# Two groups of six PSUM banks in place of three groups of four, in the second stage of a long-convolution transform

## The chip, the cores and the metric

The kernel runs on one core of one Trainium2 chip. The metric is device time in microseconds (us): from the start to the end of one execution. The engines are TensorE (PE in the profile; PEld is its weight loads), VectorE (DVE), ScalarE (ACT), GpSimd (POOL) and SyncE (SP), which issues all transfers. Matrix products go to PSUM, eight banks of 512 float32 per partition, and are copied from there to on-chip memory by ScalarE or VectorE.

## What is computed

The kernel computes the output and all gradients of a layer that adds three things: its input, a gated long convolution, and a gated bilinear unit. The sequence has 2048 tokens of 512 features, and everything is bfloat16.

```python
xn = layernorm(A_q)
k_shift = sum(pad(k)[:, t:t+S] * shift_k[:, 3-t] for t in range(4))
kv = k_shift * v
y  = irfft(rfft(kv, 2*S) * rfft(ssm_k, 2*S))[:S] + kv * ssm_D
out = A_q + xn * y + ((xn @ w_gate) * (xn @ w_up)) @ w_down
# returned: out, and its gradients by A_q, A_k, A_v, A_shift_k, A_ssm_k,
# A_ssm_D, w_gate, w_up and w_down for a given grad_out
```

The convolution over 2048 tokens needs three transforms forward: of the filter K, of kv, and of dy = xn * grad_out. Three products of these, frequency by frequency, give y, the gradient of kv and the gradient of the filter, and each of them is transformed back.

## The kernel before

**The transforms as matrix products.** Each transform is done in two stages. `a_gen` (line 432) does the first stage for all tokens, with a 64-row table, and stores the result to a scratch tensor AX. `s_gen` (line 543) then runs eight iterations over AX, two blocks each. One iteration has these parts:

- `s_load` brings in two blocks, each [128, 2, 3, 512]: the 3 are the signals t (K, kv, dy).
- `s_B(i)` (line 493) is the second forward stage. It multiplies pieces of 64 rows with tables of 64x32, for each of the two parts cp (real, imaginary), four column quarters q and two blocks s: 48 matmuls of 512 columns in all. A matmul of 64 rows and 32 columns uses an eighth of the array, so eight of them can lie side by side.
- `s_pw(2i)` and `s_pw(2i+1)` (line 508) form the three complex products on VectorE, ten operations for each block, from X (real and imaginary parts of the three signals) to Y.
- `s_Bi(i)` (line 525) is the inverse stage: three groups of 16 matmuls of 32 rows and 64 columns into four banks each, copied by ScalarE.

Later `last_dft` (line 687) does the last inverse stage.

**Groups and banks.** `rF()` asks for a tile of two adjacent banks, `rN()` for one bank. The lines between `together()` and `apart()` become a single operation for the order: the matmuls of a group are issued back to back. In `s_B` before, a group belongs to a signal t: two tiles `px[s]`, one for each block, hold its real and imaginary part, which makes four banks. Two copies empty them (line 505). ScalarE does both, except in the first iteration, where VectorE takes one of the two.

**Buffers.** There are three X tiles and six Y tiles, taken in turn: block b uses X[b % 3]. The X tile of a block is used again three blocks later.

**Other work.** Around these stages the same engines do the gated unit and its weight gradients. `mlp_rows` (line 400) forms the hidden units, with three PSUM tiles per call, each copied away. `dw_gen` (line 561) accumulates weight gradients, 16 matmuls in one bank before one copy. These matmuls stand between the groups of `s_B` and `s_Bi`.

**The order.** No scheduler runs on the chip's side. Every call is first recorded as an operation with a due time (`at`), and `emit(PLAN)` (line 181) issues all of them in an order that is written into the string PLAN, together with the bank of every PSUM tile. A planner made that string beforehand. Unpacked, it holds 2335 operation numbers and 411 bank numbers before. Each engine works through its own part of the order strictly in sequence, so a wait of one operation holds up all behind it on its engine.

Of the kernel before, what the change touches and what calls it, by code (L numbers as in the profile page):

```python
# [17 lines left out]
S = 2048  # L18
D = 512
F = 1376  # L20
R = 16
# [6 lines left out]
NCH = 8  # L28
# [1 line left out]
RING = 28  # L30
RO = [0, 16, 24, 40, 56, 72]
EPS = 1e-5
PLAN = "c-l>O0}w4u4`tF(-)GylZQHhO+qP}nwr$(C&AspYcdK@~dMcfq&dJQwbdtCLK)@iNVBjGDAs{4#g3u5K!a_WV1L+|l#E00B7;-=YKu82RAs6I@q>vkuKpqGO$ss&MfQXO}B0*$`0{Ni`M1^P&9b!NMC<v*c5EO-C5EIHnENB9SAsG~h3Q!YDKvO6QwV*Uqfs{}i%0MZo1a+V;q=l+b7V1G|XaHlNKD32~kOF!@H7Ez|U?4PtR8SEHK?`UPjbSh}gG|r?hCp@b2+46M^nsQz3_8IG=mMP~4Wz)4&<lpcRA>&Ppesy+`Opfc!)V9=-Cza$hLqSBQsE3p2P@$%^oCWi5PCvCm<fv^EA)r%Fbj^tY*++yU<s^-36L3D!x~rsYhfwOg^92p#z8n)2V-G3WQ2LJ0kXp$*aUlFJY<1wun{IhHrNNRVHxa))VLW=!U6aN$KVi5g5z)yw!>f80w*Ah{DD(&7y!4z9XJQ4;Ru|88?Xb;!d*y%h__$>T!Ni&8*aiqcmVgo;RSdDmx1sjoQJRQ4$>myMM#I~F$2B_!5sJ!a^h8Z1QGESJb^1<_z-g82bhSDVHd>4r|=oBLvDNydGHxrgN&${3BN&JoP?S26Xe4$kOi~i56Fg*F$`wM&6pp<V*!kU1+fqo#;6z$i(paoSPW}pag2sxaXLoF5;y~6U>&TB^{_rRz=jyWnAiwIVI*vfO>hfNfu`6DLt=CM4s9S7w!jy#6(?g$41sZQH@3l6*c#hnJ8X~JFf?|+jyMJ5;&vR532+B?!p^u6yI@z`i4(9J#>4K|7f)e7oQ*Sa7tX;R7$5uNN$iQou^0BnJva*o;AtF)eJ~;J#WPp~2H^o*f@g6s4#5aG4Ts`>9ENjoDxSloxCV#g2poy~@I02n1vn2E;UygHM&W2&jAL*ij&Y@NEv~?^xC~d}Sho_(U|C#^<uDPh$8|W)mB+-m2`k`u*VHv}NpOPe<St-RtcVw}r5ouwyXBY+-?`?ll`Dx8-9hZ&TDXO-nQP}-yN+&=>*?CK_HMDejJ@0vR|&6SWxR@2uqsx=D_9+CU`@R3y1QC<7jNJ=?BVWVe0Lvj<1HNJ61WHW5Fg=Ve1ZwxQ+$Tk@j1T0m-q@_;~RX7@9;f-z>jznKjCNmf?x3)E_L7W2mZuF?iVI@NnBEw%q4dzTuQghrE+)h5N^Pg?l=CyzX<LyqU-9MBgamhI&<CyTnHD^g>s=?7#G$pci~)k7r{kzkz8aK#T~(@E}Dz(Vz>-0rc3S8xU}w$%jjacOfIvl<c?xxm&FxyU0ha|&1H90++A1IRddx{4VS|ea)sRrm(CS&vE2}N&)sx6T`u<%a=ScksJrj-x_mCbi{nmUQCG~Rcg0;zH_4T7aa~Eb97?&;u8b?|%DD%wysO~myIQWctK;grimslk?~Y*s*T6k=4c%(j$h~*H-8vUmCc7zafLrVOxHWE&```w;ovxo7?E1Q?Zn)d!w!3L=y4&YwxMA*q+u>%q{cfw<?GCz+ZkF5TKDk3~j$7d7y7lh3n~#UxXE)oOc6;1Wcha43^W0;1#%*wq+$pDY)@^pT+&SlIliTR7IHMzOi~HsR#5BTPbs^}b`{MRGp-b+Sd+nmpWfzj(xC`#9i%v1<t-I*HyO@-ne!3qn2j!$(l$(CJ&~(jRcX{ZE`|ZL|JeQYNx##Yg%SZXC0EMTgE*2G}LKJ}t(+l^<MWNsULq+JXD@su*KE<X<<fyHiK#ko3nn;srCQYHR6kdu^LJCI_BoalGaTJl_QX(2p2`CvQr+ActQc@~PLW}5zn@Xvv7IkxpsWvU9g;a;?(k!Y+X{b1*rF4{@GEfXzLa`*K%%(^(hcePqiXzh~vSgxVw322}RGCMaDYitDxwMv65m9}LE~{xB9djiqu4JLC6h}%?Y05@rs4OLva#Wt;Nd>A%m8ddhl=zZB8c=_iSTajPszOz%5hayO(wH_;BB@5zDTy?pKD36iNHR$-O(~nypuW_P`cn$2NzG^gHK(kSU0P5Y$t5|YC8d&q6pB*IAR0{Rq!kUJp_G({QA)`v!zqJ|p!||nN>FPmC~YXc<d%^%ib~07Dj;pC9Tk%GG=|#K2I@dXq$72ra<Y$>Q(-AB^<+PFrY=-pHdA?NAbDg9b)~#gM!HdVDl0vxCsmNGluwFDMQI|HWE&Ni%5s2;N)>4)C1g9DcTJ_5Jfo`eoDNb$*+DO;xipfOR9#+CNqJ2*<PFu7UerR~Qf+xhz3DxDpvF>HK2jU$A!F$iIcO`N=?i_Oos^o>a4q>pX*nIYla^9Peo%L5CFwZ>XXH%WS~Bx4YA?Mc3wM;Bl9jV@Z^_R6<R^8IUo=|!N)8?)Ik}Vcmt5ROPEr>cAY-Mg43yv0S^m&pIz`=Nq6`w?$#Rs2$s|EOPRD4l<Yvc1Wt^O#AwqnHCdd?F&dXC}xQv&Xl8=RF%Lq}9L&gPpq|B00GM`S9=Q*-O3h^GAD~BjQ&y&3r;KLM>3-AtEDo5xl?UZX&mW%K%xlSwP2Hm7`e2b>Z3W>!tWSQKiJ5-qO(sH>+A^1M6l11`>D)Mw$D63^7t&xXxo+|NtStko*w_Kn{v_baDV~Wk2Bo42YxV%T=@fLYP<$1k4rF~L?FVaRiC<kP#ES9shU#8J^SwY(*6vyXFbdD16VL2p~xe7PrBXXHGOF}*>iTDZ?<%`mYL-R=~#>M%xT$03mO6v1vxgue>1SjF^a!eZV4XMk=<*Hnhq<lh>@l7eo_4t;&mUB{y@5mWR&Tl0wpOtW&g3n7zejsloJV&M%Qku(f1Wv^f`JP1LmlBz8OI3a)PvwzB;k)uqo=Z(`%<tuiJd|frop;k?iORM3gWQ)I+=M&w1^FbXZTX|r=4f1vqjM+zEbX`@e-Tp982nY*vuR(B$=`wrr2~uR;pbe3zsq;(!k4)p|B%l7OZxKw4(LE;y~3?{5dRj{Ncw{RNJxFjKP8GbXRnbptcK9RJcLbJa8!N8f8{EN)@b^aLuq(z%F*>1htr`PL&NAWZq2bZrVi(3+?BmV&{+D0zw>Lp#t}7+{@^w|g5&8(?#4YirN-6n+>29bA`M6n{>q6pjlSh1`i=YWC?3sYIJL&tvD}+K@;gqbY4ts)*94ke)9H22s5kfnXV9CRObh5IPNA9gCnwc{8bUJZ0=~t+IIG^~EV_^jX<og<`E?QJ)Wy7nKl4(~r^`5-7S`;#oO5fyis}l^p({C;hLlyjnv3XN{=&sHyshC9dXFpXeO}A!xVWz8lA1>!a1|}B5BU*~<MF(KCva5_VH3HUPU6QrnQQ12uBBzPrjnG?Iy#l>=`?1ksMC1{m(@dDNl|KR11+U9xw_8cCOVtvaCx1}b@ebG;R-sBkMgl#X>gq9b0a;$C%K`9wo_bRPxBdWrW?7jwo;Kz9LCycT06^4^&J1<kanIga0I)^zqzem;?3M%yJ%PKrrou*_RyZ%OMB}UZl}$4E4R>SwvD&*4*tt6wWIFjUBO1@u6EMh+(A{|>OJkOdw8gZmSH+vN9ai1%lr7g?&m&wfct7cJ;?oafWFg#I!GVuVBM*^bcpWOhx$bK=yQFldv%{a)BSotSLjN8p{w+uzSKv0NLTA99j#+@td7%Ac35BQ6F#D$WW2u72|7{3*(5!xuXM6b(Xh5gkLgrBu50yyp3rr=UN`7Qjc6xzlP0zVwppj^4BeuUY^$Eq(|ShFY8*SKk?p)*(5QA%FX?5yqDkzkUeoJ(LuYDI`>4t7rpB=M`bp#4ERAKeb&kfi4;t6LYjm5d^E93%vRgV|7idEJq1$x3MzMvuNEhog-JvOLiI%dImf4nS8e67WY`JE)WOiF~TL~*;sjQ-vv(i?{%Gyt@V3jSS{n9*^&Z<}@%WCPZq?u*2)Rx!0-O+s3%*tDH%WtEsl~uFxR=}!TK@-bmHLQ@;w6T`MYFS|$XFaX96|tiBS*zLv8)J3si~iQOhE~k#+H}ilf3&IfwRYCe+S?54VD+qp^|y}J)w)@Cn`Aw#flaph*2!jCL+fm6Uv-N0vTxeb2G~>^ZO$6mK$~X8t+5TVS=Pk{TN9gYZET3ev^h4^CfYC?Zu@Mh&9&Ax!uH!TTVTs=p3S#~cEDCxZ#!t~?X>l=>$c8z*<amYHw<i}ZL>u-(pK7b+hm7qv8}cpcGfoAO*?0|Y^NQzOSZ)>+8H}yw{5E(wIz1Pj@xBBW^3%cU9k*y*P{4mcEY0it9H_MTQvXN_E>a(!QNSD5B|Nqu)T)<f!(uT!BYFaJv8#K?UAwnV5dxcIDgH)*(&>JVf=Sf|Hfkawf4y(`XBb$o?0yb#bW!%_SMW+@lPzg59@zh93SxBhwyRzOAG0%`k(gJ;`u)o!&md^eF~r7NAU4|0iVGa^cj62U)?A0g?%Pp#Q(LFzNpXaBl%Rmn9uGL`Vu~o&+XIt96pp!>~s28R?{c(xqNb8#;5beeJx+oNA_8KZC}bK^>ut!U)N{zd3+6@+Sl{Re0fh+&gb>rJzIU>-&gcKd<Wm$_w)_?WMA3m^A&s=Kft%}4Sjn*(D(9Fd`I8d5AvP-RA1UR@`L>}-^6$JLwrj=)DQEO{0QI55BE*|3_sGh^)vk_-`e-~vwRmn+n4oS{d7OU&+*NCH$T_+@#FknKhKZx`}}yn-!Jp?{Q=+4xAUX@LEpyr^$Y!SzrY{z>-<)K*e~+i{1Ly{Z})5c1AojP^*j7Tf84L|>-`D8#BcBq{Yrn*Z}gA+PQS)K_N)9kf7@^JPyASa#!vE3{bqm1Kl5AsUBAmO^`HG}|J>j6r~DWH!teI?{a1h5zw$5rH-E{$_80wk|HfbTKm1!CGqA^B@gV{~eXPJ$A1(09M-Tk**L=vpZy!4lDsa|c_n`wZ0yq3$A0}|#Lx2Kd1MfTr!Uf(3Tea|k51s=Te8fP6fCO&(NP$~k191Y810THwKKUpCABY+V1V{x8nOyMi<zPN=YQg?M!Po(V8YqKf5(}DGIhe`W=|7u82qF;;gFPZB$bW_)I*5m$r{Kbr7=pc|ss*#X`=|fsG`MCFGnJq==<q*vu*HObuwe1W#uRiGEDbqGYk~qwgz|5XC<dv5^<Z$J{O=OhV9-HV!SRoV&Hk?x6iogh$cX~{NA+J6LFqp}_mB3U?DT*0KWk9?|4sf6_22lP?SI<fo&R6d8q@}Z4U#%kN9KaTss%y8Ac_7xZ;)6F{_SE5z7GZn1{PcdWBtcq!4L4yS@5_CqLJ8w-U<H?9`mRC"
KB = 1024


# [1 line left out]
def kernel(  # L38
# [39 lines left out]
    Q = [PP[:, 1024 * i:1024 * i + 1024] for i in range(4)]  # L78
    halves = [Q[i][:, 512 * h:512 * h + 512] for i in range(4) for h in range(2)]

    def v3(ap, a):
        return ap.rearrange("p (a b) -> p a b", a=a)
# [32 lines left out]
    def rF(kind="F"):  # L115
        slots.append(Slot(2, kind))
        return PV(slots[-1], lambda b: b)
# [86 lines left out]
    ACOPY = nc.scalar.copy  # L204
    VCOPY = nc.vector.tensor_copy
    MM = nc.tensor.matmul
# [37 lines left out]
    rW = Region(108 * KB, 132 * KB)  # L244
# [5 lines left out]
    W2 = W12[:, 128:192]  # L250
# [8 lines left out]
    c2 = rc.tile("c2", [128, R], F32)  # L259
# [205 lines left out]
    sp = {}  # L465

    def s_alloc():
        m = Region(RA[0] + 8 * KB, RA[1])
        sp["a"] = [m.tile(f"sa{i}", [128, 2, 3, D]) for i in range(3)]
        sp["X"] = [m.tile(f"sX{i}", [128, 3, 2, D]) for i in range(3)]  # L470
        sp["Y"] = [m.tile(f"sY{i}", [128, 2, D]) for i in range(6)]
        sp["T1"] = place([128, 2, 2, D], BF, RA[0])
        sp["T2"] = m.tile("sT2", [128, 2, 2, D])
        sp["C"] = [m.tile(f"sC{i}", [128, 2, 3, D]) for i in range(2)]
        sp["E"] = [m.tile(f"sE{i}", [128, 512]) for i in range(3)]

    def e_tab(i):
        return sp["E"][i % 3][:, 0:256].rearrange("p (g c k) -> p g c k", g=4, c=2)
# [12 lines left out]
        return 2 * s + q // 2, (q + s) % 2  # L491

    def s_B(i):
        for t in range(3):
            px = [v3(rF(), 2) for s in range(2)]
            together()
            for cp in range(2):
                for q in range(4):
                    for s in range(2):
                        g, j = s_pair(s, q)  # L500
                        h = slice(64 * j, 64 * j + 64)
                        MM(px[s][32 * q:32 * q + 32, cp, :], lhsT=e_tab(i)[h, g, cp, :], rhs=sp["a"][(2 * i + s) % 3][h, g % 2, t, :], start=True, stop=True)
            apart()
            for s in range(2):
                (VCOPY if i == 0 and s else ACOPY)(sp["X"][(2 * i + s) % 3][:, t, :, :], px[s])
            yield

    def s_pw(i):
# [50 lines left out]
    f = {}  # L559
# [228 lines left out]
    A0, AJ = 6.0, 38.0  # L788
# [3 lines left out]
    O0, OJ = 230.0, 10.0  # L792
# [60 lines left out]
    A = Gen(a_all())  # L853
# [41 lines left out]
    for n in range(NCH):  # L895
        last = n + 1 == NCH
        t = F0 + n * DF
# [138 lines left out]
```

## Time and profile before

| | before |
|---|---|
| time, median of 3 | 433.36 us (433.06 to 433.58) |
| span of the profiled execution | 1105.1 us |
| transfers | 123.07 MB, 34.4% of the DMA engines' time in the span |
| copies of 128x1024 from PSUM on ScalarE | 155, mean 1016 ns |
| copies of 128x1024 from PSUM on VectorE | 13, mean 1224 ns |

The profiled execution is one of the program on the chip, but it took 2.55 times as long as the timed ones. What it shows of a single operation of VectorE or ScalarE, and of the sequence on each engine, is of use; shares of the span have to be read with that ratio in mind. A group of instructions in the profile shows line, engine, operation and shape, then count, total busy time and the mean of one in nanoseconds, and last the idle time before these instructions with what ended it. Since a helper issues everything, all lines are line 173, and the groups are told apart by shape: 64x512 with a 64\*32 table is `s_B`, 32x512 with 32\*64 is `s_Bi`.

### The profile page before, as it was taken

The page shows a single profiled execution, that of the slowest core. Times are in us where ns is not written, and L with a number is a line of the kernel's source. Part 1 is how long each engine was busy: PE and PEld are TensorE (multiplying, and loading weights), DVE is VectorE, ACT ScalarE, POOL GpSimd, SP SyncE. Part 2 cuts the span into 40 slices and gives each one's busy share as a digit, 9 for nine tenths or more (in the row PEclk, how much of TensorE's full clock was granted, in tenths as well). Part 3 has the DMA queues.
Part 4 walks back from the last instruction along what each step waited for, and adds up shares of the span by engine and source line. Part 5 has one row for each costly group of instructions (what it writes and reads, how often), then busy time and mean ns, then how long its engine had stood idle before and what let it go on. Part 6 is the DMA issues. An engine that isn't in the chain of part 4 may idle for free.

```text
span 1105.1 us, 8192 instructions
## 1 busy us (share of the span) xinstructions
PE 1098.0 (99%) x3203; PEld 367.9 (33%) x3203; DVE 362.0 (33%) x691; ACT 275.9 (25%) x370; POOL 3.5 (0%) x9
## 2 busy tenths in 40 slices
PE   9999999999999999999999999999999999999997
PEld 5454334633333222322232224333333222232232
DVE  4324333323126142434334400111414342334333
ACT  2332233233112343333433422222111010101100
POOL 0000000000000000000000000000000000000000
DMA  9202342323503242342333338136405244335001
GB/s 340 86 29 77 119 165 109 122 110 116 201 12 143 95 152 63 100 161 72 110 138 110 110 98 189 50 119 156 126 28 157 57 124 138 103 90 175 37 29 38
DMA packets 91262, 123.07 MB, mean 111 GB/s; under 512 B 50644, under 2 KB 60249, under 8 KB 90200
## 3 DMA queue, kind: packets, MB, share of 16 engines
q1 hardware_dynamic: 91224, 122.56, 34.4%
q8 instruction: 25, 0.41, 0.2%
q14 instruction: 13, 0.11, 0.0%
HBM read 57.10 MB, written 53.25 MB: 100 GB/s over the span
## 4 chain that ended last, share of the span: by engine, by line
PE 99%; ACTq 0%; DVE 0%; DVEq 0%; ACT 0%; issue 0%
PE PP L173 99%; ACTq L1032 0%; DVE big L173 0%; DVEq L1032 0%; ACT big L173 0%; ACTq L173 0%
## 5 line engine op out<-in xcount | busy, mean ns | idle before, releaser
L173 PE MATMUL PP<-big 128*128 128x512 bf16 (+9 forms) x3203 | 1098.0, 698 | 1.1 <-DVE big L173 1.1
L173 PEld LDWEIGHTS <-big 128*128 128x128 bf16 (+5 forms) x3203 | 367.9, 149 | 730.1 <-issue 674.5
L173 DVE TENSOR_TENSOR big<-big 128x1024 bf16<-128x1024 bf16 (+3 forms) x465 | 272.0, 630 | 327.8 <-ACT big L173 257.8
L173 ACT CAST big<-PP 128x1024 bf16<-128x1024 f32 (+2 forms) x311 | 230.3, 777 | 560.0 <-PE PP L173 504.0
L173 DVE CAST big<-PP 128x512 bf16<-128x512 f32 (+1 forms) x37 | 32.5, 878 | 184.9 <-PE PP L173 135.6
L173 ACT ACTIVATE big<-big 128x512 bf16<-128x512 f32 (+3 forms) x30 | 19.0, 639 | 169.2 <-DVE big L173 169.2
L173 ACT COPY big<-PP 128x1024 bf16<-128x1024 bf16 x28 | 27.9, 1013 | 94.6 <-PE PP L173 94.6
L173 DVE SCALAR_TENSOR_TENSOR big<-big,PP 128x512 f32<-128x512 bf16 x16 | 11.0, 687 | 116.7 <-PE PP L173 116.7
L173 DVE TENSOR_TENSOR big<-big,PP 128x512 bf16<-128x512 bf16 (+1 forms) x17 | 11.1, 655 | 87.6 <-PE PP L173 87.6
L173 DVE SCALAR_TENSOR_TENSOR big<-big 128x1 f32<-128x1 f32 (+2 forms) x52 | 25.0, 498 | 0.3
L173 DVE BATCH_NORM_STATS2 big<-big 128x6 f32<-128x512 bf16 x16 | 10.6, 675 | 2.4 <-DMA big<-in_x_dram 2.4
L173 DVE TENSOR_SCALAR big<-big 128x1 f32<-128x1 f32 (+1 forms) x28 | 7.0, 260 | 0.2
L173 DVE RECIPROCAL big<-big 128x2 f32<-128x2 f32 (+1 forms) x9 | 1.3, 156 | 13.6 <-ACT big L173 13.6
L173 POOL MEMSET big<- 128x1536 bf16 (+2 forms) x3 | 2.8, 949 | 656.6 <-PE PP L173 656.6
L173 DVE BATCH_NORM_AGGREGATE big<-big 128x2 f32<-128x6 f32 x16 | 2.7, 176 | 0.1
L173 DVE COPY big<-PP 128x1024 bf16<-128x1024 bf16 x1 | 0.7, 692 | 5.0 <-PE PP L173 5.0
L173 ACT ACT_TABLE_LOAD x1 | 1.3, 1283 | 0.7 <-PEq L1024 0.7
L173 DVE DVE_READ_ACCUMULATOR big<-big,PP 128x1 f32 x16 | 1.3, 82 | 0.0
L173 DVE DVE_READ_ACCUMULATOR big<-big 128x1 f32 x16 | 1.3, 81 | 0.0
L173 DVE MEMSET big<- 128x128 bf16 (+1 forms) x2 | 0.2, 112 | 0.8 <-PEq L1024 0.8
masks.py:199 POOL TENSOR_SCALAR_AFFINE_SELECT big<-big 128x128 bf16<-128x128 bf16 x1 | 0.3, 292 | 0.0
masks.py:197 POOL MEMSET big<- 128x128 bf16 x1 | 0.2, 204 | 0.3 <-POOLq L1024 0.3
(4 smaller groups left out, 0.4 us busy)
## 6 DMA issues: line engine op xcount, KB each, us to landing
AX<-big SPq DMA_DIRECT2D x16, 768.0 KB, 4.0
big<-AX SPq DMA_DIRECT2D x16, 768.0 KB, 6.3
CX<-big SPq DMA_DIRECT2D x32, 384.0 KB, 3.9
HD<-big SPq DMA_DIRECT2D x30, 384.0 KB, 4.7
out_dram<-big SPq DMA_DIRECT2D x44, 256.0 KB, 2.5
big<-CX SPq DMA_DIRECT2D x7, 1536.0 KB, 6.4
big<-in_v_dram SPq DMA_DIRECT2D x16, 256.0 KB, 4.4
big<-in_w_dram SPq DMA_DIRECT2D x4, 768.0 KB, 6.5
```

Of the source, the lines that this page charges most:

```text
L173: o.fns.append(lambda: f(*[fix(x) for x in a], **{kk: fix(x) for kk, x in k.items()}))
```

## The change

A group of `s_B` now belongs to a part cp instead of a signal: three tiles `px[t]`, one for each signal, hold the two blocks, which makes six banks. There are two groups of 24 matmuls per iteration in place of three groups of 16. A copy empties the tile of one signal and one part and writes both blocks: the three X tiles become slices of one tile `XX`, and `both` is the slice that takes the iteration's two (with a step of -2 where the tiles are 2 and 0). In the first iteration VectorE takes signal 1 of each group, two copies in place of three.

The purpose is to have fewer and longer groups in this stage. The order and the banks of the whole kernel were planned anew: the new string holds 2327 operation numbers, eight fewer, and again 411 bank numbers.

```diff
-PLAN = "c-l>O0}w4u4`tF(-)Gy..."
+PLAN = "c-l301JGbe&u)?q`W@T0..."
...
         sp["a"] = [m.tile(f"sa{i}", [128, 2, 3, D]) for i in range(3)]
-        sp["X"] = [m.tile(f"sX{i}", [128, 3, 2, D]) for i in range(3)]
+        sp["XX"] = m.tile("sX", [128, 3, 6 * D])
+        sp["X"] = [sp["XX"][:, i].rearrange("p (t c d) -> p t c d", t=3, c=2) for i in range(3)]
...
     def s_B(i):
-        for t in range(3):
-            px = [v3(rF(), 2) for s in range(2)]
+        a, b = 2 * i % 3, (2 * i + 1) % 3
+        both = slice(a, b + 1) if b > a else slice(2, None, -2)
+        for cp in range(2):
+            px = [v3(rF(), 2) for t in range(3)]
             together()
-            for cp in range(2):
+            for t in range(3):
                 for q in range(4):
                     for s in range(2):
                         g, j = s_pair(s, q)
                         h = slice(64 * j, 64 * j + 64)
-                        MM(px[s][32 * q:32 * q + 32, cp, :], lhsT=e_tab(i)[h, g, cp, :], rhs=sp["a"][(2 * i + s) % 3][h, g % 2, t, :], start=True, stop=True)
+                        MM(px[t][32 * q:32 * q + 32, s, :], lhsT=e_tab(i)[h, g, cp, :], rhs=sp["a"][(2 * i + s) % 3][h, g % 2, t, :], start=True, stop=True)
             apart()
-            for s in range(2):
-                (VCOPY if i == 0 and s else ACOPY)(sp["X"][(2 * i + s) % 3][:, t, :, :], px[s])
+            for t in range(3):
+                (VCOPY if i == 0 and t == 1 else ACOPY)(sp["XX"][:, both, (2 * t + cp) * D:(2 * t + cp) * D + D], px[t])
             yield
```

## The prediction

> **What bounds the kernel now.** I read the page's busy times first, then the groups of instructions with shapes kept apart, then the chain of waits, then one stretch of the windows view, and last the timeline around one group of the stage that is changed.
>
> ```profile
> span 1105.1 us, 8192 instructions
> PE 1098.0 (99%) x3203; PEld 367.9 (33%) x3203; DVE 362.0 (33%) x691; ACT 275.9 (25%) x370; POOL 3.5 (0%) x9
> ```
>
> The groups (count, then busy us and mean ns of one, then the idle time before and who ended it):
>
> ```profile
> L173 PE MATMUL PP<-big 128*128 128x512 bf16 x1325 | 809.1, 828 | 1.1 <-DVE big L173 1.1
> ...
> L173 DVE TENSOR_TENSOR big<-big 128x1024 bf16<-128x1024 bf16 x246 | 163.8, 685 | 135.1 <-ACT big L173 105.9 <-PE PP L173 26.8 <-DMA KS<-big 0.6
> L173 ACT CAST big<-PP 128x1024 bf16<-128x1024 f32 x155 | 151.2, 1016 | 267.2 <-PE PP L173 239.8 <-issue 16.9 <-DVE big L173 10.2
> L173 PE MATMUL PP<-big 128*128 128x256 bf16 x358 | 114.8, 533 | 0.0
> ...
> L173 DVE TENSOR_TENSOR big<-big 128x512 bf16<-128x512 bf16 x157 | 61.9, 419 | 109.8 <-ACT big L173 70.9 <-PE PP L173 38.1
> ...
> L173 PE MATMUL PP<-big 32*64 32x512 bf16 x384 | 30.6, 738 | 0.0
> L173 PE MATMUL PP<-big 64*32 64x512 bf16 x384 | 29.7, 702 | 0.0
> ...
> L173 DVE CAST big<-PP 128x1024 bf16<-128x1024 f32 x13 | 15.9, 1224 | 69.2 <-ACT big L173 32.2 <-PE PP L173 19.9 <-issue 17.1
> ```
>
> The profiled execution took 1105.1 us, the timed ones 433.36. The profile therefore shows TensorE at a much lower speed than the timed runs have: in the start records a 128x512 matmul follows another after 0.586 us on average. Read literally, TensorE is busy 99% and nobody else matters. That can't be carried to 433 us, where VectorE's 362.0 us are 84% and ScalarE's 275.9 us are 64%. So I price TensorE anew.
>
> The groups,[...] with packed matmuls divided by the number that run side by side: 1325 x 215.8 ns = 286.0; 358 x 109.2 (256 columns) = 39.1; 240 x 55.8 (128 columns) = 13.4; 128 x 82.5 (192 columns) = 10.6; 128 x 42.5 (96 columns) = 5.4; 96 of 64 rows and 96 of 64 columns, two at a time, 20.7; 384 + 384 of the two middle stages, eight at a time, 20.7; 64 of 32 columns, four at a time, 3.5. Sum 399.4 us: 92% of 433.36. TensorE still bounds the timed kernel, but with 34 us of start, tail, tile-mode changes and waits, and VectorE is close behind.
>
> ```profile
> 1.06 1098.04 PE PP L173 x2991
> ...
> 1100.93 0.60 DVEq L1032
> ```
>
> The chain of waits is one piece of TensorE, and the last 6 us are tail that the change does not touch.
>
> ```profile
> 320.00:667.00 347.00, 347.00 (x1334) 94.22 (x1333) 125.91 (x219) 120.76 (x150) 1.47 (x2) 1.00 0.33 111
> ```
>
> This is the stretch from the first second-stage group (326 us) to the last inverse one (659 us); columns are length, then busy time of PE, PEld, DVE, ACT, POOL. TensorE's 347 us, scaled by 399.4/1098, are 126 us at the timed speed. VectorE has 125.9, ScalarE 120.8. In the stage that is changed all three engines have the same load: time taken from one returns only as far as the others wait less too.
>
> ```profile
> 440.24 0.23 PEld L173 LDWEIGHTS <-big 128*128 128x128 bf16 x1 [0.39 <-issue]
> 440.86 0.23 PEld L173 LDWEIGHTS <-big 128*128 128x128 bf16 x1 [0.39 <-issue]
> ...
> 442.19 0.14 PEld L173 LDWEIGHTS <-big 64*32 64x32 bf16 x16 [1.10 <-issue]
> ...
> 443.43 0.11 PEld L173 LDWEIGHTS <-big 128*128 128x128 bf16 x2 [1.10 <-issue]
> 443.64 1.93 ACT L173 CAST big<-PP 128x1024 bf16<-128x1024 f32 x2 [1.38 <-PE PP L173]
> ```
>
> One group of four banks: 16 matmuls in two rounds of eight, from 442.19 to 443.43, then two copies in 1.93 us. Over all 24 such groups the start records give 1.171 us from the group's first matmul to the next mode's first, which is two rounds of 0.586: leaving costs nothing. Entering does: the first matmul of a group starts 0.196 us later after the one before it than the mean spacing of that width would have it.
>
> [...]
>
> **The change part by part.**
> - *Matmuls.* 3 groups of 16 become 2 of 24: 48 matmuls and 48 weight loads per iteration as before, six rounds of eight. In a round the eight tiles still cover two row halves and four column quarters and write two banks. No difference in rounds.
> - *Entries.* One group fewer in each of 8 iterations. Unpacked, the old order changes tile mode 154 times, the new one 139 times; since only entries cost, 8 entries go. At the trace's slow engine one cost 0.196 us; if all of it scales with the clock it is 0.196 x 0.364 = 0.07; the upper end is that value unscaled[...]. I take 0.15: 8 x 0.15 = 1.2 us, range 0.6 to 1.6. This lies on TensorE's path.
> - *Copies.* Six of 128x1024 per iteration, as before. Their output becomes two runs of 512 in two X tiles. The inverse stage's copies and the first stage's write such split outputs already and take 1.016 and 1.018 us on average against 1.015 for these, so no extra cost.
> - *First iteration.* VectorE copies 2 of 6 instead of 3: -1.22 us on VectorE, +1.02 us on ScalarE. TensorE covers most of this; as VectorE is level with TensorE in the stage, I count a third, 0.4 us.
> - *X layout.* Same bytes for each row, so the 20 products per iteration cost the same.
> - *Waits.* A copy now fills both X tiles of an iteration, so it waits for the products of the earlier iteration that still read one; before, half the copies needed only the older tile. Queued behind it on ScalarE are the inverse stage's and the gated unit's copies, and for them TensorE waits with full banks. The last of three copies frees its banks after 3 x 1.016 = 3.05 us instead of 2.03. Between the two groups of an iteration the new order puts matmuls worth 10, 16, 17, 14, 14, 12, 13 and 13 times 512 columns, at 0.216 us 2.2 to 3.7 us: about as long as the copies, with two banks left for other tiles. I take it as just hidden.
> - *Order anew.* It differs from the first operations on. Cutting both orders into stretches of some 20 us and adding up the busiest engine's work in each (row durations, TensorE at the price above) gives sums within 1 us of each other: no gain or loss from it in my forecast.
>
> Sum: 433.36 - 1.2 - 0.4 = 431.8 us.
>
> **The rivals.**
> 1. *Banks become the bound: slower.* For every packed group of both middle stages I counted in the two orders the TensorE work between the last matmul into its banks and the group, less the copies started after it that free them. Less than 0.3 us is left for 13 of 48 groups before (never below 0.2), for 29 of 40 after, ten of them negative. What is missing to 0.3 us sums to 1.2 us before and 6.7 us after. If all of the difference is idle TensorE: 433.36 + 5.5 - 1.2 = 437.7. Part of it will fall into waits that exist anyway; half of it gives 434.9. I put this rival at 435.5. Against it: the shortfall of both orders counts columns only, and each entry in between adds time for the copies.
> 2. *Hidden anyway: no difference.* VectorE's 125.9 us set the stage's pace; the entries saved become waits for products. 433.3 us. Against it: VectorE loses 1.2 us too.
> 3. *More than the entries.* Entries cost 0.2 us, all of VectorE's 1.2 us counts, and with fewer groups the copies cluster better: 433.36 - 1.6 - 1.2 = 430.6, and 429 if the new order gains a little elsewhere.
>
> **How the numbers follow.** Forecast 0.35 and rival 3 0.16, together 0.51 for faster by over 0.2% (below 432.5). Rival 2 0.13. Rival 1 0.36: the count of banks is the strongest evidence against the change, and the entries the strongest for it. The range goes from 428.5 (rival 3 with some gain of the order) to 438 (rival 1 in full).
>
> **What would show it.** Right: the changed kernel has 16 entries into the 64x32 mode, rounds of the same length, 156 copies of 128x1024 on ScalarE and 12 on VectorE with the same means, and where TensorE runs at its timed speed, waits of TensorE for ScalarE in the stage no longer than before. Wrong: copies with split outputs slower than 1.02 us; weight loads or matmuls of the stage waiting for ScalarE's copies by 0.3 us and more per group (rival 1); a stage as long as before with VectorE without gaps (rival 2). If the time moves by several us with TensorE's waits in the middle stages unchanged, the order outside of them did it, and my step on the order was wrong.

## The result: slower, and what the profile after shows

| | median | runs |
|---|---|---|
| before | 433.47 us (433.06 to 434.57) | 4 |
| changed | 440.41 us (439.56 to 441.69) | 4 |

The ratio is 1.0159, with a 95% interval of 1.0126 to 1.0191: 6.9 us slower, where 1.6 us faster was forecast. The time lies above the range given.

The profile of the kernel before, which the prediction was read from, was 2.55 times as long as a timed run, so before and after can't be laid side by side. The first experiment therefore took a second profile of the unchanged kernel. It ran at the timed speed (span 430.0 us) and stands for "before" from here on. It is one execution, of 431.83 us, the changed kernel's profile one of 440.06 us: the two are 8.2 us apart where the medians are 6.9 us apart.

Before, from the page: span, busy times, share of the 16 DMA engines, the chain that ended last, TensorE's group with all shapes, and the C stores with their size and the median time from issue to landing.

```profile
span 430.0 us, 8135 instructions
...
PE 415.2 (97%) x3146; PEld 204.7 (48%) x3203; DVE 356.2 (83%) x691; ACT 267.7 (62%) x370; POOL 3.5 (1%) x9
...
q1 hardware_dynamic: 91224, 122.56, 89.8%
...
PE 86%; DVE 6%; DMA 4%; issue 2%; SPq 1%; ACT 0%; DVEq 0%
...
L173 PE MATMUL PP<-big 128*128 128x512 bf16 (+9 forms) x3146 | 415.2, 344 | 7.8 <-issue 1.6
...
CX<-big SPq DMA_DIRECT2D x32, 384.0 KB, 4.3
```

The changed kernel, same parts of its page:

```profile
span 438.3 us, 8141 instructions
...
PE 416.1 (95%) x3147; PEld 206.3 (47%) x3203; DVE 354.4 (81%) x690; ACT 267.2 (61%) x371; POOL 3.5 (1%) x9
...
q1 hardware_dynamic: 91224, 122.56, 90.1%
...
PE 61%; DMA 17%; DVE 11%; ACT 4%; issue 3%; SPq 2%; DVEq 0%; ACTq 0%
...
PE PP L173 61%; DVE big L173 11%; DMA out_dram<-big 7%; DMA CX<-big 6%; ACT big L173 4%; DMA big<-CX 3%; SPq L173 2%; DMA big<-in_goT_dram 1%; DVEq L1035 0%; ACTq L173 0%; DVEq L173 0%
...
L173 PE MATMUL PP<-big 128*128 128x512 bf16 (+9 forms) x3147 | 416.1, 344 | 14.8 <-ACT big L173 4.6
...
CX<-big SPq DMA_DIRECT2D x32, 384.0 KB, 5.1
```

Three things are to be seen. No engine has more work: the busy times differ by at most 1.8 us. TensorE's idle time goes from 7.8 to 14.8 us. And the chain tells who it waits for: TensorE's share of it falls from 86% to 61%, that of transfers rises from 4% to 17%, stores to memory (out_dram, CX) at the head. The bytes are the same; they land later. The DMA engines are busy for 90% of the span in both kernels.

By shapes (32\*64 is `s_Bi`, 64\*32 is `s_B`), before:

```profile
L173 PE MATMUL PP<-big 32*64 32x512 bf16 x384 | 15.3, 386 | 0.0
L173 PE MATMUL PP<-big 64*32 64x512 bf16 x384 | 15.1, 381 | 0.1
```

and in the changed kernel, with the copies:

```profile
L173 ACT CAST big<-PP 128x1024 bf16<-128x1024 f32 x156 | 151.3, 1028 | 47.1 <-PE PP L173 19.1 <-DMA out_dram<-big 15.3 <-DVE big L173 6.1
L173 PE MATMUL PP<-big 32*64 32x512 bf16 x384 | 16.5, 385 | 3.0 <-ACT big L173 2.9
L173 DVE CAST big<-PP 128x1024 bf16<-128x1024 f32 x12 | 14.6, 1221 | 2.8 <-PE PP L173 1.9 <-ACT big L173 0.9
L173 PE MATMUL PP<-big 64*32 64x512 bf16 x384 | 13.5, 380 | 0.0
```

The idle time ahead of `s_B`, the stage that was changed, is 0.0 us: this view shows no wait of its groups of six banks. The 3.0 us stand ahead of `s_Bi`, whose code was not touched.

A ledger makes the stages comparable. Each stage of TensorE is its length, less its matmuls at the price of the prediction, less 0.2 us for each packed group; what remains is idle time. No profile at full speed stood behind that price; the changed kernel's trace gives it. From one 128\*128 matmul to the next of its shape it has 0.216 us for 512 columns, 0.109 for 256, 0.056 for 128, 0.082 for 192 and 0.042 for 96 (medians); in the groups of `s_B` and `s_Bi` eight matmuls start 3 to 4 ns apart, and the next eight 0.216 to 0.240 us after the first. The 0.2 us are read from the traces at full speed: 0.09 us on entering (a group's first matmul starts 0.309 us after a 128x512 one, where the next of the same shape starts after 0.216), and from a group of 24's first matmul to the next mode's 0.775 us at the median where three rounds are 0.648, so some 0.13 on leaving.

| idle TensorE, us | head, to the first `s_B` | S stage, to the last `s_Bi` | to the first last_dft | last stage | sum |
|---|---|---|---|---|---|
| before | 5.8 | 1.8 | 0.2 | -0.3 | 7.5 |
| changed | 5.5 | 6.5 | 1.4 | 3.7 | 17.1 |

That is 9.6 us more idle, less 8 x 0.2 = 1.6 us for the groups saved: 8.0 us, against 8.3 us between the spans. The expectation of the first experiment, below, had 6 to 8 us in the middle stages for banks and under 3 us for the order; 4.7 us in the S stage is neither. The loss has two seats, the S stage (4.7 us) and what follows it (5.2 us). Orders that agree in the head differ there by up to 1.5 us from profile to profile, so single entries of the table are good to about that.

**The S stage.** The chain of waits around its worst place (start us, us, what):

```profile
226.13 7.67 DMA CX<-big
...
234.82 2.01 ACT big L173 x3
...
236.87 2.27 PE PP L173 x28
```

Each of an iteration's two blocks has one C tile, used again in every iteration. ScalarE's copy of `s_Bi` into it may not overwrite what an earlier iteration's store (CX<-big) still reads; that store lands at 233.8, the copy starts, TensorE waits for it. Why it lands late stands in SyncE's list (start us, us, what):

```profile
221.37 2.09 SPq L173 DMA_DIRECT2D CX<-big  x3
223.55 1.02 SPq L173 DMA_DIRECT2D big<-in_tab_dram  x1
224.67 1.42 SPq L173 DMA_DIRECT2D big<-in_wy_dram  x1
226.13 0.53 SPq L173 DMA_DIRECT2D CX<-big  x1
```

The iteration's fourth store is issued behind a table load and the 768 KB of wy. In the order before, the four stores of this iteration stood together.

**After the S stage.** SyncE again:

```profile
265.81 3.29 SPq L173 DMA_DIRECT2D CX<-big  x4
269.21 10.03 SPq L173 DMA_TRANSPOSE big<-HD  x1
279.43 0.50 SPq L173 DMA_DIRECT2D big<-CX  x1
```

and the chain from there on:

```profile
279.43 4.23 DMA big<-CX
...
283.70 1.50 PE PP L173 x12
...
285.23 9.17 DMA big<-CX
...
294.44 1.81 PE PP L173 x13
```

A transposing load holds SyncE for 10.0 us. Behind it stands the last load of C rows (big<-CX), which the first last_dft needs; after that one the next rows can be loaded, and the second last_dft waits for them too. The order before has the same load behind the same transposing load:

```profile
264.88 9.14 SPq L173 DMA_TRANSPOSE big<-HD  x1
274.23 0.50 SPq L173 DMA_DIRECT2D big<-CX  x1
```

There it costs next to nothing (0.2 us in the ledger): TensorE has 18.3 us of matmuls from the last `s_Bi` to the first last_dft, in the changed kernel 17.8, and the transposing load holds SyncE 0.9 us less. So the place behind it is no difference between the two orders; how long it holds, and how much work covers it, is. Later in the chain:

```profile
326.07 4.11 DVE big L173 x8
...
330.99 5.03 DMA out_dram<-big
...
336.11 0.20 DVE big L173
```

Here the queue holds nothing up for long. VectorE finishes a product, its store leaves 0.8 us later and takes 5.0 us, and VectorE's next writing of the same single tile (that of `dk_pair`) stands so close behind that it waits, and ScalarE and TensorE's `y_o` behind it.

In these lists nothing leaves SyncE before the transfer ahead of it has been issued: 10.0 us for the one behind the transposing load at 269.2. The view of waits puts 24.0 us of its time from 262 to 345 us down to TensorE, in five waits; 21.7 us of them, in three, lie within the records of transposing loads, where waiting and loading are not told apart. Nothing behind them is issued meanwhile. Before, it is 27.1 us in seven waits: the waiting itself is not new, what stands behind it is.

### The profile page after: what moved, and what is told of

Its sections match the earlier page's. It is cut to its first block, busy times and chain, and to the rows that moved or that the text cites. A ratio compares the mean times of both kernels' runs of the same rounds, so it can differ in the third digit from the quotient of the medians.

```text
span 438.3 us, 8141 instructions
## 1 busy us (share of the span) xinstructions
PE 416.1 (95%) x3147; PEld 206.3 (47%) x3203; DVE 354.4 (81%) x690; ACT 267.2 (61%) x371; POOL 3.5 (1%) x9
## 4 chain that ended last, share of the span: by engine, by line
PE 61%; DMA 17%; DVE 11%; ACT 4%; issue 3%; SPq 2%; DVEq 0%; ACTq 0%
PE PP L173 61%; DVE big L173 11%; DMA out_dram<-big 7%; DMA CX<-big 6%; ACT big L173 4%; DMA big<-CX 3%; SPq L173 2%; DMA big<-in_goT_dram 1%; DVEq L1035 0%; ACTq L173 0%; DVEq L173 0%
## 5 line engine op out<-in xcount | busy, mean ns | idle before, releaser
L173 PE MATMUL PP<-big 128*128 128x512 bf16 (+9 forms) x3147 | 416.1, 344 | 14.8 <-ACT big L173 4.6
L173 DVE TENSOR_TENSOR big<-big 128x1024 bf16<-128x1024 bf16 (+4 forms) x465 | 270.4, 631 | 53.9 <-ACT big L173 38.7
L173 PEld LDWEIGHTS <-big 128*128 128x128 bf16 (+5 forms) x3203 | 206.3, 98 | 224.2 <-issue 62.3
L173 ACT CAST big<-PP 128x1024 bf16<-128x1024 f32 (+3 forms) x312 | 222.8, 790 | 83.3 <-PE PP L173 44.4
L173 DVE CAST big<-PP 128x512 bf16<-128x512 f32 (+1 forms) x36 | 30.8, 866 | 11.8 <-PE PP L173 9.6
```

Of the source, the lines that this page charges most:

```text
L173: o.fns.append(lambda: f(*[fix(x) for x in a], **{kk: fix(x) for kk, x in k.items()}))
```

## The experiments

Two theories. *Order*: the loss is made by the order that was planned anew, by where transfers stand in the queue and by what waits for them, close behind; the groups of six are neutral but for the 1.6 us they save. *Grouping* (called "banks" in the first expectations): six banks at once starve the other tiles, whatever the order. Where only the order is changed, the diff shows the list that PLAN holds.

**The kernel before, once more**

> The kernel before, unchanged, to have it in a profile at the speed of the timed runs. If the banks set the pace after the change (theory: banks), TensorE here waits for ScalarE's and VectorE's copies by some 6 to 8 us less in the middle stages than the 440 us kernel does, and the stretches outside of them are equal within 1 us. If the new order as a whole is at fault (theory: order), the middle stages differ by less than 3 us and the head or the tail carries the rest. Entries into a packed mode should cost 0.08 us here as in the changed kernel.

431.83 us, and the profile above. Entering a packed mode costs 0.09 us in it as in the changed kernel.

**Four stores side by side.** Changed kernel; five of SyncE's transfers issued later, in three iterations, such as this one:

```diff
 store C, 3rd
-load table
-load wy (768 KB)
 store C, 4th
+load table
+load wy (768 KB)
```

> The changed kernel with five of SyncE's transfers moved: in each iteration the four stores of the inverse stage to CX are issued one after the other, and the loads or stores that stood between them come after the fourth. All else is as in the changed kernel. If late transfers are the cause (theory: transfers), the copies of the inverse stage wait less for these stores, the TensorE stalls of 1.04 and 0.37 us at about 235 us go, and the time falls by 1 to 1.5 us, to about 439. If the banks are (theory: banks), the stalls stay where they are and the time is 440.4 within 0.5.

437.62 us (436.65 to 439.2), ratio 1.0094 (1.0065 to 1.0123): 2.8 us back, about twice what was expected. Waits of TensorE for ScalarE and of ScalarE for the C store in the S stage (128 to 264 us; in total, times, longest), changed kernel:

```profile
ACT big L173 <- DMA CX<-big: 5.0, 4, 1.9
PE PP L173 <- ACT big L173: 3.1, 7, 1.0
```

and with the stores together:

```profile
PE PP L173 <- ACT big L173: 0.7, 4, 0.2
...
ACT big L173 <- DMA CX<-big: 0.2, 1, 0.2
```

The wait for the store is gone, and with it TensorE's. S stage idle 6.5 to 3.6 us. Groups and banks are the same in both.

**The mirror: stores apart in the kernel before.** Groups of four; four stores issued later, in two iterations (the expectation counts five):

```diff
 store C, 1st
-store C, 2nd to 4th
 load table
 load s
+store C, 2nd to 4th
...
 store C, 3rd
-store C, 4th
 load wy (768 KB)
 load table
+store C, 4th
```

> The kernel before, with only five transfers of the S stage issued later: in the second iteration three of the four stores of the C tile behind two small loads, in the fifth the last store behind the 768 KB load of wy and the table load, as in the changed kernel. Theory 'order': ScalarE's next copy into the C tile waits for the late store, TensorE for it, 1.5 to 3 us more, 435 to 436.5 us. Theory 'grouping': no change, 433 to 434 us.

442.23 us (439.96 to 444.24), ratio 1.0211 (1.0168 to 1.0253): 9.4 us slower, three times the expectation. One place holds half of it (chain of waits):

```profile
170.93 4.27 PE PP L173 x49
...
175.60 0.52 SPq L173
...
176.18 6.16 DMA CX<-big
...
182.44 1.02 ACT big L173
...
183.50 3.32 PE PP L173 x20
```

The load of s, now ahead of the stores, waits itself until TensorE has done with its tile: SyncE issues no transfer from 170.4 to 175.2 us. The stores wait behind it, the copy behind the store, and TensorE stands still for 4.4 us.

A second part of the loss is not waiting. The page gives TensorE's busy time and the clock granted to it, in 40 slices of 11.0 us, in tenths:

```profile
PE   7899999999999999599989999999999999999993
PEclk9999999999999999799999999999999999999998
```

The trace has the clock at half from 181.3 to 188.1 us, from within that wait to 4.6 us after it. 128x512 matmuls follow one another after 0.426 us there instead of 0.216, so these 4.6 us do the work of 2.3. Before, and in the changed kernel, the clock stays full from the first 4 us to the tail (in the changed kernel's trace from 3.8 to 433.9 us). Another 1.2 us are one wait for a table load. The S stage's idle time, in which the ledger counts the slow clock too, goes from 1.8 to 10.4 us: 4.4 us of it are the wait for the store, 2.3 the clock, 1.2 the table. The mean granted clock is low in all four executions, 0.983 to 0.988 where the kernel before had 0.995 to 0.998. The expectation had asked for 1.5 to 3 us of waiting and for nothing else. So four misplaced stores, with what follows from them, cost more than the whole change, without a group of six.

**The mirror of the last stage.** Kernel before, groups of four; from the last `s_Bi` on, all engines in the order of the changed kernel.

> The mirror: the kernel before, with its three groups of four, and from the last inverse transform of the S stage on, every engine's order and SyncE's transfers as in the changed kernel (five PSUM tiles in another bank). Theory 'order': the changed kernel's waits of the last stage appear here, 3 to 5 us more idle TensorE there, 436.5 to 438.5 us. Theory 'grouping': 433 to 434.5 us, as before.

435.74 us (435.36 to 436.78), ratio 1.0069 (1.0047 to 1.009): 2.9 us slower, a little under the expectation. The same wait appears as in the changed kernel:

```profile
322.01 3.92 DVE big L173 x8
325.94 6.08 DMA out_dram<-big
...
334.12 1.02 ACT big L173
...
335.19 3.40 PE PP L173 x15
```

The theory of grouping wanted no change in either mirror. It falls as an account of these losses.

**The last stage of the kernel before in the changed one.** Stores together, groups of six; from the last `s_Bi` on, the order of the kernel before (662 operations).

> The changed kernel with the four stores of the C tile side by side (437.62 us), and from the last inverse transform of the S stage on, every engine's order and SyncE's transfers as in the kernel before (662 operations; four of the tiles in PSUM in another bank). The six-bank groups stay. Theory 'order': the last stage's idle time of TensorE goes from about 3.6 us to under 0.5, so 433.5 to 435 us. Theory 'grouping': the loss is made in the S stage and stays, so 437 us or more.

436.85 us (436.3 to 437.36), ratio 1.0088 (1.0065 to 1.011). Only 0.8 us back, which is not clear of the noise, and short of both figures. The last stage's idle time falls from 3.0 to 2.1 us, but that ahead of the first last_dft rises from 0.6 to 1.3: the order before relied on 18.3 us of matmuls ahead of it, and the S stage of the changed kernel leaves 16.7. A piece of a planned order is not worth the same elsewhere.

**The transposing load later.** As the last one, and one transfer moved:

```diff
-transposing load of HD
 load C rows, 4th
 store out
 load wy
 load x
 load x
+transposing load of HD
```

> The changed kernel with the four stores side by side and the last stage in the order of the kernel before (436.85 us), and one transfer moved: the first transposing load of the last stage, which holds SyncE for 8.6 us, goes behind the five transfers that stood queued behind it (the last C rows, a store, the load of wy and two of x). Theory 'order': TensorE's waits of 1.06, 1.11 and 0.73 us around the first inverse transform of that stage shrink to under 1 us together; 434.3 to 435.8 us. Theory 'grouping': what is left of the loss has nothing to do with this queue; 436.5 us or more.

436.57 us (434.87 to 439.98), ratio 1.0092 (1.0061 to 1.0123): by the times no difference, in a spread of 5 us. In the trace the idle time ahead of the first last_dft goes from 1.3 to 0.3 us as expected, but the wait moves on to the second: TensorE waits there 1.4 us for C rows. The times don't settle it: they lie just inside the figure of grouping, not in that of order.

**Three operations of the last stage moved.** Stores together, two groups of `y_o` ahead of the second last_dft, one `dk_pair` product twelve places earlier on VectorE.

> The changed kernel with the stores side by side (437.62 us), and three operations of the last stage in another place: two groups of four matmuls of y_o ahead of the second inverse transform of that stage on TensorE (1.7 us of other work while its C rows land), and one product of dk_pair twelve operations earlier on VectorE, so that the store it ends in leaves earlier. Transfers' order, banks and groups of six stay. Theory 'order': the two waits that TensorE's list shows there in that kernel's own trace (1.48 us ahead of last_dft, 1.26 us ahead of y_o) shrink to under 0.5 us each; 435 to 436.3 us. Theory 'grouping': nothing in it depends on these places: 437 us or more.

437.44 us (435.84 to 438.07), ratio 1.008 (1.0053 to 1.0108): no difference, as grouping had it. The wait ahead of the second last_dft is gone, that ahead of `y_o` stays at 1.43 us, and one of 1.37 us appears ahead of `y_x`. The wait was displaced.

**Orders searched anew.** Six kernels, the PLAN string alone, in which an annealing search over a model of the kernel looked for a better order. Two with the transfers' order free and all else fixed, in the changed kernel and as a control in the kernel before:

> The changed kernel with SyncE's transfers in another order throughout; the orders of TensorE, VectorE and ScalarE and all banks are the changed kernel's. Transfers: 3 to 4 us come back, 436 to 437.5, from the waits for stores to CX in the middle and for loads and stores held up behind the transposing loads at the end. Banks: 440 within 0.7, since no bank and no copy has moved.

438.07 us (437.12 to 441.45), ratio 1.0115 (1.007 to 1.0159): between the two figures.

> The kernel before with SyncE's transfers in another order, found in the same way as that of the run on the changed kernel. A control: if it gains as much as that run (3 us or more), the gain there says nothing about the change. Transfers: at most 2 us, 431.5 to 433.5, since only 0.6 us of TensorE's waits are for transfers after the start. Banks: no statement, 433 within 1.

435.66 us (433.71 to 437.15), ratio 1.0047 (1.0028 to 1.0066). The search makes the kernel before 2 us slower, which neither figure had. The changed kernel's median falls by 2.3 us, but the two intervals (1.0126 to 1.0191 and 1.007 to 1.0159) overlap, so that gain is not clear of the noise.

Two with everything free, groups of six and groups of four:

> Two groups of six banks as in the changed kernel, but the order of all engines and the banks chosen anew, with the transfers' landing times of the traces taken into account. Banks: six of eight banks in one hand keep TensorE waiting in any order, 436 or more. Transfers: the grouping itself is harmless and its 8 entries less are worth 1.6 us, so 433 or below.

437.41 us (436.54 to 437.88), ratio 1.0081 (1.0056 to 1.0107). By the figure banks was right (436 or more), by its reason not, as the waits below show.

> Control to the full re-search of the changed kernel (437.41 us): the three groups of four of the kernel before, with the order of all engines and the banks searched anew in the same way and for as long. Theory 'order' (what costs is the place of the transfers and what stands behind them, the grouping is neutral): a search that does not know the transfers well is no better here, so 436 to 438 us, within 1.5 us of the same search with six-bank groups. Theory 'grouping' (six-bank groups starve the banks): no more than 434.5 us, 3 us or more below it.

439.07 us (437.83 to 443.89), ratio 1.016 (1.0097 to 1.0223). Treated alike, in one search each, groups of six come out no worse than groups of four; both are slower than the kernel before. Order's figure is missed by 1 us, grouping's by over 4. The waits of TensorE in the S stage, with six:

```profile
PE PP L173 <- DVE big L173: 0.2, 1, 0.2
```

and with four:

```profile
PE PP L173 <- DVE big L173: 1.7, 5, 0.6
PE PP L173 <- issue: 1.6, 10, 0.2
PE PP L173 <- ACT big L173: 0.3, 2, 0.2
```

Six-bank groups can stand in this stage with 0.2 us of waits for other engines. By the ledger the stage has 3.2 us of idle time with six banks and 6.0 with four, against 1.8 in the kernel before.

Two more kept the transfers' order, and the search used the landing times of each kernel's own trace:

> The changed kernel with two groups of six and the transfers in exactly the order of the one with the stores side by side (437.62 us); the order on TensorE, VectorE and ScalarE and the banks searched anew against the times that each transfer took to land in that kernel's own trace. The search's own sum of durations goes from 434.9 us of span to 422.9 us. Theory 'order': with the copies and matmuls placed where the transfers have landed, the idle time of TensorE after the head goes from 7.2 to under 3 us, and the kernel to 431 to 434 us. Theory 'grouping': whatever stands around it, groups of six lose to groups of four: 436 us or more, and 3 us or more above the kernel of the next expectation.

444.14 us (441.85 to 445.52), ratio 1.0242 (1.0212 to 1.0273).

> Control: the kernel before with its three groups of four, its transfers in their own order, and the other engines' order and the banks searched anew in the same way, for as long, against the landing times of its own trace. The search's own sum goes from 429.6 to 425.5 us of span. Theory 'order': its idle time outside the head is only 1.7 us, so little is left to gain: 431 to 434 us, within 1.5 us of the kernel with groups of six treated alike, which carries eight changes of tile shape less (1.6 us). Theory 'grouping': 430 to 433 us, 3 us or more below that kernel.

438.5 us (437.51 to 439.17), ratio 1.0118 (1.0092 to 1.0144). Both are some 6 and 5 us slower than the orders they started from, where the search promised 12 and 4 us. The theory of order missed both its figures. Grouping's came true for the first kernel (over 436 us, and over 3 us above the second) and not for the second. In the first the idle time of the last stage is 11.9 us: TensorE waits for loads again (2.7 us for C rows, 2.2 us for HD), and its clock is at half in three stretches of 3.4 us that begin after stalls of 2.2 to 2.5 us, which costs up to 5 us more (mean granted clock 0.985 in this execution). In the second the last matmul ends at 426.4 us of a span of 436.2; behind it lie 2.8 us more than in the kernel before. Landing times are not constants of a transfer: the C stores' median is 4.3 us before and 5.1 us in the changed kernel. That an order fitted to them changes them in turn is the author's reading, not shown by a figure of these two traces. The times of this pair don't speak for grouping all the same: its largest difference, 11.6 us of idle time, lies in the last stage, where both kernels have the same groups. In the S stage, where the groups differ, the idle time is 4.2 us with six banks and 4.5 with four, TensorE's waits for ScalarE and VectorE 2.2 and 0.4.

Idle TensorE of the kernels with a small edit, as in the ledger above:

| | head | S stage | to last_dft | last stage |
|---|---|---|---|---|
| changed, stores together | 6.5 | 3.6 | 0.6 | 3.0 |
| same, last stage of before | 6.8 | 3.8 | 1.3 | 2.1 |
| same, transposing load later | 6.4 | 3.6 | 0.3 | 1.8 |
| before, stores apart | 6.2 | 10.4 | 0.4 | 1.1 |
| before, last stage of changed | 6.2 | 1.6 | 1.2 | 2.1 |

Four kernels with groups of six (the full search, the retimed one, the three moves, the load later) ended where grouping had put them, in their times. In their traces TensorE waits for ScalarE and VectorE by only 0.2 to 2.2 us in the S stage (0.5 in the kernel before), and the larger waits lie behind it. So what speaks against grouping in these four is the reading of traces, not a test.

## Why the prediction was wrong

The step that failed is "Order anew: no gain or loss from it in my forecast". It compared the work of three engines in stretches of 20 us and left out the fourth queue. SyncE's transfers were moved as well, and in the S stage their place is what costs: with the four C stores put back together 2.8 of the 6.9 us return, the S stage's idle time falls by 2.9 us, and the kernel before loses 9.4 us when its stores are parted (some 2.3 us of them by the clock). After the S stage it is the order of all engines together: moved into the kernel before, it costs 2.9 us. The way back, in the changed kernel, brought no gain clear of the noise, and which of its parts costs how much was not separated.

The error began with the reading of the page. In a span of 1105 us the transfers filled 34.4% of the DMA engines' time, which looks like room. The prediction rescaled TensorE to the timed speed and forgot to rescale the rest: 34.4% x 1105.1/433.36 = 88%, and the second profile shows 89.8%. A share of 88% is a reason to ask what stands behind what in SyncE's list.

The other steps, one by one:

- *Entries*: right in direction, small in size. Eight groups fewer, each 0.2 us instead of 0.15: 1.6 us, not 1.2. "Leaving costs nothing" held only at the slow TensorE of that profile; at full speed leaving takes some 0.13 us and entering 0.09. The sum is about the 0.196 us of the slow profile, so it hardly scaled with the speed, where the prediction let it scale in part.
- *Matmuls and first iteration*: counts as said (384 + 384, 156 and 12 copies). Whether the 0.4 us for the first iteration came is not seen in any run.
- *Copies*: those of `s_B` take 1.035 us instead of 1.020, above the bound that was named as a refutation. But the copies of `s_Bi`, which the change did not touch, go from 1.018 to 1.035 as well, and in the fully searched order with six banks all 156 average 1.022. So the split output is not shown to be what they pay for. Together 94 x 0.016 = 1.5 us on ScalarE, which is busy for 61%.
- *Waits, just hidden*: right where it was placed. Nothing waits ahead of `s_B`.
- *Rival 1, banks*: right in the symptom (slower, TensorE waiting for ScalarE in the middle stages), wrong in the cause. The copies were late for a store, not for want of banks: the waits left when five transfers were moved and no bank was.
- *Times carried over from the slow profile*: right for VectorE and ScalarE, 362.0 and 275.9 us of work there and 356.2 and 267.7 at full speed.
- *VectorE level with TensorE*: in the S stage at full speed VectorE has 121.6 us of work in 133.6 and TensorE 128.1, so VectorE does not set the pace.

What stays open: the best kernels with groups of six end 3 to 4 us above the kernel before, though they carry 1.6 us less of group changes. The traces of those with a small edit put it into small idle times in the S stage (about 2 us more) and after it (2 to 4 us more), after it mostly waits for C rows or for stores. That this is the order alone is not shown: an effect of the six-bank groups on what stands around them is not excluded for it. Whether an order exists in which groups of six beat 433 us was not found. Doubling the C tile or the tile of `dk_pair`, so that a copy need not wait for the store before, was not tried.

## What to carry to other kernels

Where an order is planned anew along with a change, compare the list of transfers of the two orders as carefully as the engines: look for a store that frees a tile and now stands behind a large load or one that itself waits, and for a second writing of a tile close behind its store. Rescale the DMA share with the span before calling transfers free. And judge a local change in such a kernel with the order of all else held fixed; here the place of the C stores was worth 2.8 us in one kernel and 9.4 us in the other. Look at the granted clock before putting a whole loss down to a wait.

## What the runs showed that was not expected

- A transposing load holds SyncE for 7.8 to 12.5 us in the changed kernel (eight of them, median 9.4), and for 7.6 to 9.9 us before; meanwhile nothing else leaves that queue. Its own data land 10.5 to 12.4 us after issue in the changed kernel.
- Leaving a packed tile mode costs about 0.13 us at full speed, more than entering it (0.09). In the profile with the slow TensorE it was 0.196 us on entering and nothing on leaving: some 0.2 us for both together at either speed.
- After some stalls TensorE ran at half its clock: for 6.8 us in the kernel before with its stores apart, where the stall took 4.4 us, and three times for 3.4 us in the changed kernel with the retimed order, after stalls of 2.2 to 2.5 us. In the fully searched order with six banks a stall of 2.4 us was followed by no slow clock (mean granted clock 0.997), so the length of the stall alone does not tell.
- Landing times answer to the order: the 384 KB stores of the C tile took 4.3 us at the median before and 5.1 us after, with the same bytes. With the stores side by side in the changed kernel it was 4.5, with the stores apart in the kernel before 5.1 (one profiled execution each).
